# Reordering the opening and the hand-written slots of a sliding-window attention plus feed-forward kernel

## The chip, the cores and the metric

The kernel runs on one core of one Trainium2 chip. The metric is the device time of one execution in microseconds (us), shown as the median of several runs. One execution was also taken by the hardware profiler; all views below come from it. TensorE does the matmuls and weight loads, VectorE the masks, norms and statistics, ScalarE the exponentials, most casts and most of the ReLUs, GpSimd (POOL in the profile) and SyncE (SP) issue transfers.

## What is computed

```
q, k, v: [8, 8, 576, 64] fp32        # batch, heads, sequence, head size
rel    = pos[:, None] - pos[None, :]
scores = q @ k^T / sqrt(64) - slope[h] * |rel|, kept where 0 <= rel < 128
x      = softmax(scores) @ v, heads side by side -> [8, 576, 512]
xn     = (x - mean(x)) / sqrt(var(x) + 1e-6) * g_ln
out    = x + relu(xn @ w_ch1) @ w_ch2      # 512 -> 2048 -> 512, fp32 out
```

## The kernel before

The attention goes over 8 sequences ("b") of 4 head pairs ("hp") each, 32 pairs numbered n = 4b + hp. One pair needs its q, k and v in fp32 staging tiles (four deep, so pair n + 4 reuses the tile of pair n), a cast of each to fp16, and a transpose of q and k. For the pairs n below 10 (`PE_TURNS`) the transpose is a TensorE transpose (`turn_pe`) and a VectorE copy out of PSUM (`turn_out`); from pair 10 on it is a DMA transpose on the SP queue (`turn_dma`, L184). Then come two groups of score matmuls (`scores`, L249), an exponential for each group on ScalarE (`expo`), a multiplication with the decayed band mask on VectorE (`mask`), the product with v for each of the two heads (`pv`, L291) and the division by the row sum (`norm`). In the first sequence the second group's scores go to two single banks, and its exponential is two instructions.

After a sequence's fourth pair, five token blocks are normalised: `stats` (two VectorE instructions), `rstd` (two small ScalarE instructions), `scaled` (VectorE, L362, tile xs), and a transpose into the tile xt, on TensorE for sequences 0 and 1 (`xturn_pe`, copied out by ScalarE at L387) and by DMA on SP afterwards (`xturn_dma`, L374).

The feed-forward part goes over 9 chunks of 512 tokens. A chunk is 16 groups of four matmuls `m1` (L397, each followed by `relu`, every fourth one on VectorE) and 16 groups of four matmuls `m2` (L418, with `finish` adding x and storing). Chunk c needs xt of all its tokens: chunk 0 those of sequence 0, chunk 1 reaches into block 3 of sequence 1, chunks 2 and 3 reach into block 2 of sequences 2 and 3, chunks 4 and 5 into block 1 of sequences 4 and 5.

The order of the work is written by hand. Every operation is given a slot number through `at(t, fn, ...)`; one slot is about one group of four `m1` or `m2` matmuls. The list is sorted by slot and emitted inside `tc.manual_schedule()`, and each engine and queue executes its share in that order. `T0` is the slot of the first `m1`; `base(n)` is the slot at which pair n's scores start, and the other steps of the pair stand at fixed distances from it; `lead` is how many slots ahead of it the q and k casts stand. Slots set the order alone: an instruction starts when those ahead of it on its engine are done and its inputs are there.

The opening loads of the kernel before are outside that region, in the text ahead of it. There the order on a queue is chosen by the framework's scheduler: on the GpSimd queue the first quarter of W1 (`load_w1(0)`) and the tails of the second sequence's q and k came out ahead of the first sequence's v, and the rest of the second sequence's first pairs was mixed in between. The v loads carry an added dependency (`gated`) on the k load of their pair. Each load is two DMAs of 128 KB (tails one of 128 KB); each quarter of W1 and W2 is one of 512 KB in fp16. The GpSimd queue has eight completion semaphores, so that a DMA waits for the eighth before it to land.

`scale_w1` multiplies W1 by the gain g_ln in place, in 16 pieces.

Of the kernel before, what the change touches and what calls it, by code (L numbers as in the profile page):

```python
# [16 lines left out]
def kernel(  # L17
# [10 lines left out]
    nc = tc.nc  # L28
    B, H, S, D = q.shape
# [15 lines left out]
    inv_sqrt_d = float(1.0 / np.sqrt(D))  # L45
    eps = 1e-6
# [73 lines left out]
    def gated(d, gate):  # L120
        if gate is not None:
            tc.add_manual_dep(d.ins, gate.ins.name, SYNC, reason="load order")
        return d

    def load(n, b, hp, eng, gate=None):
        for g in range(2):
            d = eng.dma_start(  # L127
                out=stage[n][(b * HPAIRS + hp) % NSTG][:, :, g, :],
                in_=dram[n][b, 2 * hp + g, 0 : NFULL * P, :].rearrange("(sb p) d -> p sb d", p=P),
            )  # L130
            gated(d, gate)
        return d

    def load_tail(n, b, eng, gate=None):
        d = eng.dma_start(
            out=stage_t[n][b % 2][:, :, :],
            in_=dram[n][b, :, NFULL * P : S, :].rearrange("h p d -> p h d"),
        )
        return gated(d, gate)

    def load_w1(i):
        f0 = i * 512
        nc.gpsimd.dma_start(out=w1sb[:, :, f0 : f0 + 512], in_=w1r[:, :, f0 : f0 + 512])
# [297 lines left out]
    def at(t, fn, *args):  # L441
        todo.append((t, len(todo), fn, args))

    T0 = 29.5
    LAST = B * HPAIRS
    PE_TURNS = 2 * HPAIRS + 2

    def base(n):
        b, hp = divmod(n, HPAIRS)
        if b == 0:  # L450
            return 6.5 + 3.8 * hp
        if b == 1:
# [6 lines left out]
    nc.vector.memset(eps_t, eps)  # L459
    for i in range(2):  # L460
        nc.vector.memset(tail16["k"][i][TAIL:P, :, :], 0.0)
        nc.vector.memset(vext[i][:, :, :, D:VD], 1.0)
        nc.vector.memset(vext[i][TAIL:P, NSB - 1, :, :], 0.0)


    nc.scalar.dma_start(out=iden, in_=iden_dram.ap())
    kgate = {0: load("k", 0, 0, nc.scalar)}
    load_tail("k", 0, nc.scalar)
    nc.scalar.preload_act_table_set("natural_log_exp_and_others")
    load("q", 0, 0, nc.sync)  # L470
    load_tail("q", 0, nc.sync)
    for hp in range(HPAIRS):
        hs = slice(2 * hp, 2 * hp + 2)
        if hp > 0:
            load("q", 0, hp, nc.sync)
            kgate[hp] = load("k", 0, hp, nc.sync)
        nc.sync.dma_start(out=masks[:, hs, :], in_=m_dram.ap()[:, hs, :])
    nc.sync.dma_start(out=g_sb, in_=moe_g_ln.rearrange("(kb p) -> p kb", p=P))
    for hp in range(HPAIRS):
        load("v", 0, hp, nc.gpsimd, kgate[hp])  # L480
        if hp == 0:
            load_tail("v", 0, nc.gpsimd, kgate[hp])
    load_w1(0)

    def load_seq(b, hp):
        if hp == 0:
# [17 lines left out]
    for n in range(LAST):  # L504
        b, hp = divmod(n, HPAIRS)
        a = base(n)
        first = b == 0
        if hp == 0:
            at(a - 9.0, new_batch, b)
        if first:  # L510
            at(a - 2.2, cast, "q", b, hp, nc.scalar)
            at(a - 2.1, cast, "k", b, hp, nc.vector if hp == 0 else nc.scalar)
            ops = (-1.4, -1.0, -0.9, -0.5, -0.4)
            at(a + 1.95, cast_v, b, hp, nc.scalar)
            if hp == 0:
                at(a + 1.96, cast_v_tail, b, nc.scalar)
            e = (0.0, 0.3, 0.2, 1.0, 1.7, 2.7, 3.5, 3.7, 3.6, 3.9)
        else:
            lead = 3.6 if n < PE_TURNS else 8.0
            at(a - lead, cast, "q", b, hp, nc.scalar)  # L520
            at(a - lead + 0.05, cast, "k", b, hp, nc.vector)
            ops = (-2.4, -1.7, -3.5, -2.0, -1.3)
            at(a - 3.0, cast_v, b, hp, nc.scalar)
            if hp == 0:
                at(a - 2.95, cast_v_tail, b, nc.scalar)
            e = (0.0, 0.5, 2.6, 3.1, 2.0, 4.6, 6.3, 6.8, 7.2, 7.7)
        for x, m in ((0.0, "q"), (0.1, "k")):
            if n < PE_TURNS:
                at(a + ops[0] + x, turn_pe, m, b, hp)
                at(a + ops[1] + x, turn_out, m, b, hp)  # L530
            else:
                at(a - lead + 0.6 + x, turn_dma, m, b, hp)
            if hp == 0:
                teng = nc.scalar if m == "q" else nc.vector
                if n < PE_TURNS:
                    at(a + ops[2] + x, cast_tail, m, b, teng)
                    at(a + ops[3] + x, turn_tail_pe, m, b)
                    at(a + ops[4] + x, turn_tail_out, m, b)
                else:
                    at(a - lead + 0.1 + x, cast_tail, m, b, teng)  # L540
                    at(a - lead + 0.8 + x, turn_tail_dma, m, b)
        at(a + e[0], scores, b, hp, 0, False)
        at(a + e[1], expo, b, hp, 0, False)
        at(a + e[2], scores, b, hp, 1, first)
        at(a + e[3], expo, b, hp, 1, first)
        at(a + e[4], mask, b, hp, 0)
        at(a + e[5], mask, b, hp, 1)
        at(a + e[6], pv, b, hp, 0)
        at(a + e[7], norm, b, hp, 0)
        at(a + e[8], pv, b, hp, 1)  # L550
        at(a + e[9], norm, b, hp, 1)
        if hp == HPAIRS - 1:
            s = a + e[9] + 0.6
            if b % 2 == 1:
                at(s, move_half, b)
            u = 0.8 if first else 1.0
            for tb in range(NSB):
                at(s + u * tb, stats, b, tb)
                x = s + u * (2.9, 3.3, 4.9, 5.3, 6.0)[tb]
                at(x, scaled, b, tb)  # L560
                at(x + 0.3, xturn_pe if b <= 1 else xturn_dma, b, tb)
            at(s + u * 2.1, rstd, b, 0, 2)
            at(s + u * 4.1, rstd, b, 2, 4)
            at(s + u * 5.1, rstd, b, 4, 5)

    for c in range(NCHUNK):
        w = T0 + (NFB + 4 * CBLK) * c
        for fb in range(NFB):
            at(w + fb, m1, c, fb)
            at(w + fb + 0.95, relu, c, fb)  # L570
        for i in range(4 * CBLK):
            tb, f0 = divmod(i, 4)
            if c == 0:
                f0, tb = divmod(i, CBLK)
            at(w + NFB + i, m2, c, tb, 4 * f0)
            if f0 == 3:
                at(w + NFB + i + 0.95, finish, c, tb)
# [34 lines left out]
```

## Time and profile before

| | us |
|---|---|
| median of 13 runs | 377.44 |
| lowest and highest of them | 374.28, 380.69 |
| the profiled execution, its own time | 379.91 |
| span in its trace, first to last instruction | 378.1 |
| TensorE busy | 320.2 |
| VectorE busy | 202.9 |
| ScalarE busy | 190.6 |
| first `m1` matmul starts at | 48.6 |
| first `m1` of chunk 1, 2, 3, 4, 5 | 94.1, 138.1, 178.75, 215.3, 253.3 |

The profiled execution took 2.47 us more than the median of the runs. Of its own time 1.8 us lie outside the span. In the timeline a row is one instruction, or several alike that follow each other: start, duration, engine, line, operation, output and inputs, shapes, count, and in brackets the idle time of the engine before it with what ended it. The table by stretches gives, for each, its length and the busy time of each engine, then the mean clock granted to TensorE (1.00 is full speed), the mean busy share of the DMA engines and the rate that they moved.

### The profile page before, as it was taken

Reading aid. Unit: us, or ns where it says so; the run is one execution under the profiler, and the core shown is the slowest. Engines: PE = TensorE matmul, PEld = TensorE weight load, DVE = VectorE, ACT = ScalarE, POOL = GpSimd, SP = SyncE. Lnnn points to the kernel's source line nnn. Section 1 sums busy time; section 2 is a strip of 40 time slices with the busy share of each in tenths; the row PEclk is TensorE's granted clock in tenths of the full one; section 3 lists DMA queues with packets and bytes.
Section 4 is the critical chain, followed back from the end, with each engine's and each line's share of the span. In section 5 each row is a group of like instructions: output and inputs, shape, how many; then the busy total and the mean of one; then the engine's idle time right before and its main releaser. Section 6 shows DMA issues by size and latency. Waiting matters only on the chain.

```text
span 378.1 us, 6132 instructions
## 1 busy us (share of the span) xinstructions
PE 320.2 (85%) x2256; PEld 155.5 (41%) x2256; DVE 202.9 (54%) x460; ACT 190.6 (50%) x329; POOL 153.3 (41%) x210
## 2 busy tenths in 40 slices
PE   0354299986998949996999899969999999999995
PEld 0243144543444414442444344424444444444442
DVE  1456737667564935585366855855586557221221
ACT  2356769534785327741675477427745722511500
POOL 2739943795758334834366448344100000000000
PEclk9996579999899989997899999999999999999999
DMA  8997699669889993699469987997345106202002
GB/s 153 215 216 196 161 202 210 161 189 239 181 147 153 211 208 101 138 196 229 122 150 191 205 192 146 216 215 165 88 114 132 29 28 134 76 28 85 0 28 85
DMA packets 73309, 56.09 MB, mean 148 GB/s; under 512 B 57216, under 2 KB 61312, under 8 KB 73280
## 3 DMA queue, kind: packets, MB, share of 16 engines
q0 software_dynamic: 13728, 30.16, 38.9%
q1 hardware_dynamic: 57824, 25.12, 32.6%
q10 hardware_dynamic: 1728, 0.43, 0.7%
q8 instruction: 18, 0.29, 0.4%
q14 instruction: 11, 0.09, 0.1%
HBM read 37.78 MB, written 9.44 MB: 125 GB/s over the span
## 4 chain that ended last, share of the span: by engine, by line
PE 58%; DMA 18%; DVE 12%; POOL 3%; issue 3%; SPq 2%; ACT 2%; ACTq 0%; POOLq 0%
PE pm L397 31%; PE po L418 19%; DMA xt<-xs 6%; DMA kT<-k 5%; DVE st L333 4%; PE sc L249 3%; PE ppv L291 3%; DMA kt<-in_k_dram 3%; DMA w1sb<-in_moe_w_ch_dram 2%; DMA k<-in_k_dram 2%; DVE o L429 2%; DVE xs L362 2%; DVE pr L280 1%; SPq L127 1%; POOL v L127 1%
## 5 line engine op out<-in xcount | busy, mean ns | idle before, releaser
L397 PE MATMUL pm<-xt,w1sb 128*128 128x512 f16 x576 | 139.4, 390 | 8.7 <-DMA xt<-xs 8.7
L418 PE MATMUL po<-w2sb,ht 128*128 128x512 f16 x576 | 134.6, 382 | 0.0
L408 ACT ACTIVATE ht<-pm 128x512 f16<-128x512 f32 x108 | 64.4, 599 | 71.3 <-PE pm L397 71.2
L267 ACT ACTIVATE pr<-sc 128x1024 f16<-128x1024 f32 x60 | 61.4, 1023 | 47.1 <-PE sc L249 46.9
L397 PEld LDWEIGHTS <-w1sb 128*128 128x128 f16 x576 | 53.3, 99 | 73.2 <-issue 12.9
L418 PEld LDWEIGHTS <-ht 128*128 128x128 f16 x576 | 53.0, 98 | 60.7 <-issue 3.5
L127 POOL DMA_DIRECT2D v<-in_v_dram x64 | 47.7, 749 | 72.4 <-ACT vx L160 52.1
L280 DVE TENSOR_TENSOR pr<-pr,masks 128x1024 f16<-128x1024 f16 x64 | 43.8, 684 | 29.6 <-ACT pr L267 28.4
L127 POOL DMA_DIRECT2D k<-in_k_dram x56 | 41.8, 751 | 22.9 <-DVE k L162 16.8
L410 DVE TENSOR_SCALAR ht<-pm 128x512 f16<-128x512 f32 x36 | 24.9, 691 | 46.9 <-PE pm L397 46.7
L127 POOL DMA_DIRECT2D q<-in_q_dram x56 | 41.9, 753 | 16.0 <-ACT q L160 10.0
L429 DVE TENSOR_TENSOR o<-po,xp 128x512 f32<-128x512 f32 x36 | 24.6, 684 | 29.9 <-PE po L418 28.3
L291 PEld LDWEIGHTS <-pr 128*128 128x128 f16 x576 | 27.3, 101 | 20.7 <-DVE pr L280 4.2
L291 PE MATMUL ppv<-vx,pr 128*128 128x65 f16 x576 | 29.7, 198 | 6.5 <-ACT vx L160 4.3
L249 PE MATMUL sc<-qT,kT 64*128 64x256 f16 x240 | 23.4, 276 | 7.3 <-DMA kT<-k 7.1
L304 DVE RECIPROCAL rec<-ppv 128x5 f32<-128x5 f32 x64 | 12.2, 191 | 27.6 <-PE ppv L291 27.5
L339 ACT ACTIVATE rstd<-mv,eps_t 128x2 f32<-128x2 f32 (+1 forms) x24 | 7.0, 294 | 31.0 <-DVE mv L334 30.8
L249 PEld LDWEIGHTS <-kT 64*128 64x128 f16 x320 | 11.6, 100 | 25.1 <-issue 13.6
L160 ACT ACTIVATE q<-q 128x512 f16<-128x512 f32 x32 | 20.1, 627 | 2.6 <-DMA q<-in_q_dram 2.4
L160 ACT ACTIVATE vx<-v 128x512 f16<-128x512 f32 x32 | 20.0, 626 | 0.9 <-DMA v<-in_v_dram 0.9
L200 PE MATMUL ptr<-iden,q 128*128 128x128 f16 x40 | 4.8, 254 | 15.4 <-ACT q L160 15.4
L162 DVE CAST k<-k 128x512 f16<-128x512 f32 x29 | 12.5, 432 | 9.0 <-DMA k<-in_k_dram 9.0
(49 smaller groups left out, 198.8 us busy)
## 6 DMA issues: line engine op xcount, KB each, us to landing
out_dram<-o SPq DMA_DIRECT2D x36, 256.0 KB, 2.7
v<-in_v_dram POOLq DMA_DIRECT2D x64, 128.0 KB, 4.2
q<-in_q_dram POOLq DMA_DIRECT2D x56, 128.0 KB, 4.8
k<-in_k_dram POOLq DMA_DIRECT2D x56, 128.0 KB, 4.5
w1sb<-in_moe_w_ch_dram POOLq DMA_DIRECT2D x4, 512.0 KB, 8.3
w2sb<-in_moe_w_ch_dram POOLq DMA_DIRECT2D x4, 512.0 KB, 15.3
xp<-xo SPq DMA_DIRECT2D x4, 320.0 KB, 5.1
q<-in_q_dram SPq DMA_DIRECT2D x8, 128.0 KB, 7.8
```

The source lines that it names most:

```text
L127: d = eng.dma_start(out=stage[n][(b * HPAIRS + hp) % NSTG][:, :, g, :], in_=dram[n][b, 2 * hp + g, 0 : NFULL * P, :].rearrange("(sb p) d - ...
L160: nc.scalar.activation(out=out_, in_=in_, func=AF.Copy)
L249: nc.tensor.matmul(sc[g][:, OFF[j] + c0 : OFF[j] + c0 + n], kt[r, q0 : q0 + P] if j < NFULL else ktl[r, hp, :], src[r, col : col + n] if c ...
L267: nc.scalar.activation(out=pr[:, :, :], in_=c16_of.pop("sc")[:, :, :], func=AF.Exp, scale=inv_sqrt_d)
L280: nc.vector.tensor_tensor(out=view, in0=view, in1=m, op=ALU.mult)
L291: nc.tensor.matmul(ppv[:, qb, :], pr_of[b, hp, GRP[j]][:, g, off : off + P], vx[:, j, h, 0 : D + 1], start=(j == qb), stop=(j == max(qb - ...
L333: nc.vector.bn_stats(out=st[0:r, :], in_=xb_of[b][0:r, tb, :])
L397: nc.tensor.matmul(pm[:, :], w1sb[:, kb, fb * P : fb * P + P], xts[c][:, kb, :], start=(kb == 0), stop=(kb == NKB - 1),)
L408: nc.scalar.activation(out=hts[c][:, fb, :], in_=pm[:, :], func=AF.Relu)
L410: nc.vector.tensor_scalar(out=hts[c][:, fb, :], in0=pm[:, :], scalar1=0.0, scalar2=None, op0=ALU.max)
L418: nc.tensor.matmul(pms[c, "o", tb][:, :], hts[c][:, fb, tb * P : tb * P + P], w2sb[:, fb, :], start=(fb == 0), stop=(fb == NFB - 1),)
L429: nc.vector.tensor_tensor(out=o_tile[:, :], in0=pms.pop((c, "o", tb))[:, :], in1=xp_of[blk // PBLK][:, blk % PBLK, :], op=ALU.add,)
```

## The change

The opening loads and memsets become a function `opening()` at slot -100, so that they too are emitted in the written order. On the GpSimd queue this gives: v of all four pairs of the first sequence, each behind its k; all four quarters of W1; then the second sequence; then W2 as before. The q and k casts and the turns of the first sequence move up by 1.5 slots, which on ScalarE puts the casts of pair n + 1 ahead of the exponentials of pair n, and on TensorE its turns ahead of the `pv` of pair n. The v casts of pairs 1 and 3 of the first sequence go to VectorE; the second sequence's k casts go from VectorE to ScalarE. The first quarter of W1 is scaled on VectorE, behind the normalisation of the first sequence, instead of on ScalarE in the middle of it.

The second sequence's attention starts 5 slots later and is spaced 4.7 instead of 5.2 slots; the third's is spaced 5.5 instead of 6.5; from the fourth on the attention stands half a slot later. Every chunk from 1 on stands 2.5 slots later (`chunk_at`). `lead` for the pairs that are turned by DMA goes from 8 to 11 slots: the casts on ScalarE and VectorE and both DMA transposes on SP move up with it, ahead of the third and fourth xt transposes of the sequence that is being normalised. The normalisation of sequences 0 and 1 gets a denser order. The number and size of the instructions of each kind stay the same, apart from the casts and scalings that change their engine.

```diff
-    T0 = 29.5
+    T0 = 29.0
...
         if b == 0:
-            return 6.5 + 3.8 * hp
+            return 6.0 + 3.8 * hp
         if b == 1:
-            return T0 + 2.0 + 5.2 * hp
+            return T0 + 7.5 + 4.7 * hp
         if b == 2:
-            return T0 + 29.0 + 6.5 * hp
-        return T0 - 42.0 + 8.0 * n
+            return T0 + 30.5 + 5.5 * hp
+        return T0 - 41.0 + 8.0 * n
+
+    def chunk_at(c):
+        return T0 + (NFB + 4 * CBLK) * c + (3.0 if c else 0.0)
+
+    def opening():
...
+        for hp in range(HPAIRS):
+            load("v", 0, hp, nc.gpsimd, kgate[hp])
+            if hp == 0:
+                load_tail("v", 0, nc.gpsimd, kgate[hp])
+        for i in range(4):
+            load_w1(i)
+
+    at(-100.0, opening)
...
-    for i in range(1, 4):
-        at(base(HPAIRS - 1) + 2.1 + 0.01 * i, load_w1, i)
...
-            t = T0 - 5.0 if i == 0 else T0 - 1.2 + 3.45 * i
-            at(t + 0.1 * kb, scale_w1, i, kb, nc.scalar if i == 0 or kb % 2 else nc.vector)
+            t = T0 - 0.35 if i == 0 else T0 - 1.0 + 3.45 * i
+            at(t + 0.05 * kb, scale_w1, i, kb, nc.scalar if i and kb % 2 else nc.vector)
...
         if first:
-            at(a - 2.2, cast, "q", b, hp, nc.scalar)
-            at(a - 2.1, cast, "k", b, hp, nc.vector if hp == 0 else nc.scalar)
-            ops = (-1.4, -1.0, -0.9, -0.5, -0.4)
-            at(a + 1.95, cast_v, b, hp, nc.scalar)
+            at(a - 3.7, cast, "q", b, hp, nc.scalar)
+            at(a - 3.6, cast, "k", b, hp, nc.vector if hp == 0 else nc.scalar)
+            ops = (-2.9, -2.6, -2.4, -2.0, -1.9)
+            at(a + 1.3, cast_v, b, hp, nc.scalar if hp % 2 == 0 else nc.vector)
...
-            lead = 3.6 if n < PE_TURNS else 8.0
+            lead = 3.6 if n < PE_TURNS else 11.0
             at(a - lead, cast, "q", b, hp, nc.scalar)
-            at(a - lead + 0.05, cast, "k", b, hp, nc.vector)
+            at(a - lead + 0.05, cast, "k", b, hp, nc.scalar if b == 1 else nc.vector)
...
-            u = 0.8 if first else 1.0
+            if b <= 1:
+                st, sc, rs = (0.0, 0.8, 1.6, 2.5, 5.0), (2.0, 3.0, 3.3, 3.6, 6.0), (1.7, 2.95, 5.9)
+            else:
+                u = 1.0
+                st = [u * x for x in (0.0, 1.0, 2.0, 3.0, 4.0)]
+                sc = [u * x for x in (2.9, 3.3, 4.9, 5.3, 6.0)]
+                rs = [u * x for x in (2.1, 4.1, 5.1)]
...
-        w = T0 + (NFB + 4 * CBLK) * c
+        w = chunk_at(c)
```

More of the change, by code (lines that the diff above doesn't have):

```diff
@@ L450, in base @@
         if b == 0:
-            return 6.5 + 3.8 * hp
+            return 6.0 + 3.8 * hp
         if b == 1:
-            return T0 + 2.0 + 5.2 * hp
+            return T0 + 7.5 + 4.7 * hp
         if b == 2:
-            return T0 + 29.0 + 6.5 * hp
-        return T0 - 42.0 + 8.0 * n
[L459 to L463, printed above, removed]
@@ L466 @@
[L466 to L477, printed above, removed]
@@ L478 @@
[L478 to L483, printed above, removed]
+            return T0 + 30.5 + 5.5 * hp
[3 more added lines that the diff above has]
+    def opening():
+        nc.vector.memset(eps_t, eps)
+        for i in range(2):
+            nc.vector.memset(tail16["k"][i][TAIL:P, :, :], 0.0)
+            nc.vector.memset(vext[i][:, :, :, D:VD], 1.0)
+            nc.vector.memset(vext[i][TAIL:P, NSB - 1, :, :], 0.0)
+        nc.scalar.dma_start(out=iden, in_=iden_dram.ap())
+        kgate = {0: load("k", 0, 0, nc.scalar)}
+        load_tail("k", 0, nc.scalar)
+        nc.scalar.preload_act_table_set("natural_log_exp_and_others")
+        load("q", 0, 0, nc.sync)
+        load_tail("q", 0, nc.sync)
+        for hp in range(HPAIRS):
+            hs = slice(2 * hp, 2 * hp + 2)
+            if hp > 0:
+                load("q", 0, hp, nc.sync)
+                kgate[hp] = load("k", 0, hp, nc.sync)
+            nc.sync.dma_start(out=masks[:, hs, :], in_=m_dram.ap()[:, hs, :])
+        nc.sync.dma_start(out=g_sb, in_=moe_g_ln.rearrange("(kb p) -> p kb", p=P))
+        for hp in range(HPAIRS):
+            load("v", 0, hp, nc.gpsimd, kgate[hp])
[3 more added lines that the diff above has]
+            load_w1(i)
@@ L510 @@
         if first:
[L511 to L514 removed]
+            at(a - 3.7, cast, "q", b, hp, nc.scalar)
+            at(a - 3.6, cast, "k", b, hp, nc.vector if hp == 0 else nc.scalar)
+            ops = (-2.9, -2.6, -2.4, -2.0, -1.9)
+            at(a + 1.3, cast_v, b, hp, nc.scalar if hp % 2 == 0 else nc.vector)
             if hp == 0:
[L516 removed]
+                at(a + 1.35, cast_v_tail, b, nc.scalar)
             e = (0.0, 0.3, 0.2, 1.0, 1.7, 2.7, 3.5, 3.7, 3.6, 3.9)
         else:
[L519 removed]
+            lead = 3.6 if n < PE_TURNS else 11.0
             at(a - lead, cast, "q", b, hp, nc.scalar)
[L521 removed]
+            at(a - lead + 0.05, cast, "k", b, hp, nc.scalar if b == 1 else nc.vector)
             ops = (-2.4, -1.7, -3.5, -2.0, -1.3)
@@ L555 @@
                 at(s, move_half, b)
-            u = 0.8 if first else 1.0
-            for tb in range(NSB):
[L558 to L564, printed above, removed]
+            if b <= 1:
[5 more added lines that the diff above has]
+                rs = [u * x for x in (2.1, 4.1, 5.1)]
+            for tb in range(NSB):
+                at(s + st[tb], stats, b, tb)
+                at(s + sc[tb], scaled, b, tb)
+                at(s + sc[tb] + 0.3, xturn_pe if b <= 1 else xturn_dma, b, tb)
+            for x, c0, c1 in zip(rs, (0, 2, 4), (2, 4, 5)):
+                at(s + x, rstd, b, c0, c1)
     for c in range(NCHUNK):
-        w = T0 + (NFB + 4 * CBLK) * c
+        w = chunk_at(c)
         for fb in range(NFB):
```

## The prediction

> **What bounds the kernel now.** I read the page's slices first, then the chain of waits, then the table by stretches, then the timeline where a stretch is longer than its work.
>
> ```profile
> PE   0354299986998949996999899969999999999995
> PEclk9996579999899989997899999999999999999999
> L397 PE MATMUL pm<-xt,w1sb 128*128 128x512 f16 x576 | 139.4, 390 | 8.7 <-DMA xt<-xs 8.7
> ```
>
> TensorE is nearly full from slice 6 on, except for dips that come once per chunk, and several of these are followed by a dip of the clock. Ahead of slice 6 it is mostly idle. So there are two places to win: the 48.6 us ahead of the first `m1`, and the dips.
>
> ```profile
> 94.10:138.10 44.00, 36.60 (x287) 17.45 (x284) 27.46 (x62) 25.00 (x43) 27.35 (x37) 0.97 1.00 183
> 138.10:178.75 40.65, 36.12 (x249) 16.52 (x249) 22.58 (x51) 21.31 (x36) 18.77 (x26) 0.92 0.83 165
> 178.75:215.31 36.56, 35.14 (x249) 16.42 (x249) 22.15 (x51) 21.32 (x36) 19.84 (x27) 0.95 0.86 165
> 215.31:253.26 37.95, 33.81 (x249) 16.06 (x249) 23.75 (x55) 21.26 (x36) 20.08 (x27) 1.00 1.00 190
> 253.26:287.60 34.34, 33.74 (x250) 16.35 (x251) 22.74 (x53) 21.15 (x36) 7.43 (x10) 1.00 0.57 129
> ```
>
> Each row runs from one chunk's first `m1` to the next. The last four hold the same TensorE work, but take 40.65, 36.56, 37.95 and 34.34 us. The last, at full clock with 0.6 us idle, gives the clean length: 33.74. The first row has one `pv` pair, two turns and an xt turn more (0.54 + 0.46 + 0.23), so 35.0. The losses are 9.0, 6.9, 2.8, 4.2 and 0.6: **23.5 us**. From 287.6 to 318.9 TensorE is busy for 31.30 of 31.30 us, and behind that only matmuls run: nothing can be won there.
>
> ```profile
> 120.84 0.39 PE L249 MATMUL sc<-qT,kT 64*128 64x256 f16 x4 [1.13 <-DMA kT<-k]
> 138.08 1.86 PE L397 MATMUL pm<-xt,w1sb 128*128 128x512 f16 x4 [5.23 <-DMA xt<-xs]
> 174.21 0.39 PE L249 MATMUL sc<-qT,kT 64*128 64x256 f16 x4 [2.23 <-DMA kT<-k]
> 178.75 1.89 PE L397 MATMUL pm<-xt,w1sb 128*128 128x512 f16 x4 [1.31 <-DMA xt<-xs]
> 249.34 0.39 PE L249 MATMUL sc<-qT,kT 64*128 64x256 f16 x4 [1.78 <-DMA kT<-k]
> 253.26 1.04 PE L397 MATMUL pm<-xt,w1sb 128*128 128x512 f16 x4 [1.70 <-DMA xt<-xs]
> ```
>
> The losses are waits for DMA transposes of k and of xs (in all 7.1 and 8.7 us). The groups at 138.08 and 178.75 take 1.86 and 1.89 us where the one at 253.26 takes 1.04: there the clock is at half speed.
>
> **The change, part 1: the opening.** In the timeline of the first sequence, ScalarE and GpSimd show these rows:
>
> ```profile
> 28.06 1.02 ACT L267 ACTIVATE pr<-sc 128x1024 f16<-128x1024 f32 x1 [1.78 <-PE sc L249]
> 28.98 1.08 ACT L263 ACTIVATE pr<-sch 128x512 f16<-128x512 f32 x2
> 29.20 1.49 POOL L127 DMA_DIRECT2D v<-in_v_dram  x2 [2.40 <-DMA k<-in_k_dram]
> 29.94 0.64 ACT L160 ACTIVATE q<-q 128x512 f16<-128x512 f32 x1
> 40.12 2.54 ACT L152 ACTIVATE w1sb<-w1sb,g_sb 128x512 f16<-128x512 f16 x4
> ```
>
> Pair 3's casts stand behind pair 2's exponentials, its turns behind its casts, and pair 2's `pv` behind those turns. Scores start at 14.4, 22.1, 27.4 and 32.6. With casts and turns ahead, a pair costs 0.65 (scores) + 2.1 (exponentials) + 0.7 (mask) + 0.9 (rest of `pv`), 4.3 us, instead of 5.2, if its loads are there. They set the pace: each exponential now also waits for the next pair's k. GpSimd's waits show k of pairs 1, 2, 3 landing at 15.2, 23.1 and 29.2. By then W1's first quarter (0.52 MB) and tails of sequence 2 (0.26 MB) had passed, and for the last two also its third tail and parts of its first pair (0.52 MB more). The stretches show 203 to 230 GB/s; at 217 these 0.78 and 1.30 MB are 3.6 and 6.0 us. So k lands at 11.6, 17.1 and 23.2 at the latest; the last by bytes at 22.7, which I take. Then: two casts, 1.2 us (23.9); pair 2's exponentials (26.0); mask (26.7); `pv`; pair 3's scores at 27.6. From scores to `stats` was 32.6 to 37.95, 5.35 us, less 0.15 with the v cast on VectorE: 32.8.
>
> From `stats` to the first `m1` was 10.7 us, with the 2.54 us of W1 scaling shown above in the middle of it on ScalarE, and casts and turns of sequence 2 at its end. Now: three `stats` (0.82 each), `rstd` (0.5), two `scaled` (0.42), wait for the second `rstd`, two `scaled`, about 5.5 us; transposes, copies and the last small block, to 8.0; the first W1 piece, 0.35. First `m1` at 32.8 + 8.4 = 41.2: **7.4 us gained**. W1 is issued behind v of pair 3, from about 24.5, with 2.1 MB landing by some 36; not late.
>
> Sequence 2's loads now wait behind W1 on GpSimd's queue and semaphores, from about 36.5, at 0.75 us per DMA. Its first q and k land near 40; their casts stand behind three `m1` groups, at 45. W2 is issued near 50 (46.6 before); its first quarter is wanted after sixteen groups, above 60. Both cost nothing; if this cover failed, the delay would be theirs in full, 2 to 5 us.
>
> A rule speaks against moving casts and scalings to VectorE. W1's four issues took 0.75 to 1.06 us each on GpSimd (median 0.84), partly beside VectorE's casts, W2's four 0.76 to 0.79. The Trainium skill ("SBUF — State Buffer", "Who interferes with whom") says that a VectorE copy or scaling in a two-port mode shuts GpSimd out for the whole instruction. By the rule the two v casts (0.43 each) and four scalings (0.35) add up to 2.3 us to the queue; by the rows, at most 0.3 for each, 1.8. Either is inside the slack of the paragraph above: I add nothing, with 2.3 kept for the range.
>
> **Part 2: chunk 0.** The stretch from first `m1` to chunk 1's took 45.5 us. It takes over the turns of sequence 2's first pair with its tails (0.9) and those of the third sequence's second pair (0.5). ScalarE takes four k casts more (0.64 each) beside 12 ReLUs; it was 94% busy from 60 to 70 us, so I add 1.3, between 0 and 2.6. At the end, the last `pv` used to be followed by 8.7 us of TensorE work in 13.7 us; now by three `m2` groups, scores, turns and xt turns, 4.6, while VectorE has 8.4 us of norm, four `stats`, four `scaled`, three `finish` and a mask, then about 2 us for the last turn and copy: idle 5.8 instead of 5.0, so 0.8. Sum **3.5 us lost**.
>
> **Part 3: chunks 1 to 5.** The chunks move 2.5 slots back, the attention half a slot: two slots more between xs and its chunk, and 4.5 for chunk 2. A slot is 0.86 us, with the attention between about 1.05. The chain from the last `pv` of a sequence to xt's landing is about 14 us; TensorE now has 13 us of work for it, against 8 at chunk 2 and 11 at chunk 3. Remainders: 1.4 at chunks 2 and 3, 0.7 at chunk 5. The DMA transposes of q and k stand 3 slots earlier; the waits for them were 0.8 to 2.2 us, so they go. They are moved past the third or fourth xt transpose on SP (1.2 us to issue each), which no chunk is waiting for next. Casts standing earlier on ScalarE must find their loads there: the load of a pair waits for a cast some 30 slots ahead of it and takes 4.8 us to land, so they do. Waits for masks stay, 2.0.
>
> Half clock is the last term. By the stretch of 178 to 182 us the granted clock was 0.50, and it had fallen in 174 to 178 (0.66) behind an idle of only 2.23. The skill ("TensorE: Matmul & The Clock Gate", "What's actually happening") has the gate fall to half after an idle window of about 3.4 us. By the rule remainders of 1.4 us never cost clock; by the rows they may. I take one such stretch, 1.3 us (1.86 for 1.04, and the next group's part); the rule would make it 0.
>
> What is left is 1.4 + 1.4 + 0.7 + 2.0 + 1.3 = 6.8 of 23.5; with the 0.5 of turns that moved ahead, **17.2 us gained**.
>
> **Sum**: -7.4 + 3.5 - 17.2 = -21.1 us. The profiled execution's 379.9 becomes 358.8; it stood 2.5 above the median of the runs, so against 377.4 the kernel takes **356 us**.
>
> **The rivals.**
> *The opening stays bound by issue, not bytes.* SP's own issues wait for space (2.0 to 4.05 us for some masks and loads), so k of pair 3 could land at 27 in spite of fewer bytes. Then `m1` starts near 46 and 2.5 of the 7.4 us are left: 361. For it: SP's long issues[...].
> *The stalls come back at the chunks.* With k's waits gone TensorE arrives earlier and waits for xt instead; VectorE is busy for 12.2 of 20 us there, in one piece. If half of the 23.5 remain, 5 us more than I leave: 361 to 366.
> *Slower: ScalarE blocked by early casts.* 22 pairs' q casts stand three slots earlier, ahead of ReLUs and exponentials. If a load is not there, ScalarE stops, PSUM fills and TensorE with it, up to three slots (2.6 us) per pair, 57 us: 413. It decides from 1 us per pair on, 21 us, which eats the gain. Against it: the trace shows only 2.4 us of q casts waiting for loads, all at the first pair.
>
> **How the numbers follow.** My forecast 0.70 (348 to 362 alone), the opening's rival 0.12, the stalls' 0.12, the slower one 0.05; 0.01 that gains and losses cancel. The range 346 to 367 takes in the first three with the 2.3, 2.6 and 5 us of the unknown costs; outside it lie the slower case and the rest of the tails. About 0.3% is what a measurement of this kernel can tell from no change. Faster 0.93, same 0.01, slower 0.06.
>
> **What would show it.** Right: first `m1` near 41, no wait for kT above 0.5 us, waits for xt at chunks 2 and 3 under 2 us, stretches between chunks of 34 to 36 us. Wrong: a first `m1` behind 46, q casts that wait for loads on ScalarE, stretches that stay at 38 or more, or W2's first quarter holding the first `m2`.

## The result, and the profile after

The changed kernel takes 365.7 us (median of 11 runs, 362.3 to 373.6) against 377.4 us for the kernel before in the same comparison: a ratio of 0.968 [0.965, 0.971], 11.7 us less. Ratios here leave out executions over 1.5% above the fastest of their kernel. The forecast was 356 us, 21.4 less, so little more than half of the forecast gain came. The range up to 367 held the time with 1.3 us to spare; it lies outside the 348 to 362 that the prediction gave to its own account alone.

The profiled pair shows more. The changed kernel's profiled execution took 362.81 us, 2.9 below its median; that of before took 379.91, 2.5 above. So the two traces lie 17.1 us apart (spans 378.1 and 361.0), the medians 11.7. Both differences need an explanation, and they have different ones.

The slices and the costliest group on the changed kernel's page:

```profile
PE   1662789995999998998999999989999999999995
PEclk9999999996799999999999999999999999999999
L397 PE MATMUL pm<-xt,w1sb 128*128 128x512 f16 x576 | 137.0, 386 | 2.1 <-DMA xt<-xs 1.5
```

TensorE is at work from slice 5 on instead of slice 6. The one deep dip left is slice 10, the end of chunk 0, and there and in slice 11 the clock still falls (0.6 and 0.7). The waits for xt shrank from 8.7 to 1.5 us.

The changed kernel's table by stretches (length, busy time of PE, PEld, DVE, ACT and POOL, granted clock, DMA share, GB/s), from one chunk's first `m1` to the next, chunks 0 to 5. The DMA share adds up the times of all packets; they overlap, so it can pass 1.00.

```profile
39.75:91.00 51.25, 43.96 (x340) 22.55 (x341) 32.69 (x76) 33.84 (x59) 41.39 (x56) 0.93 0.92 200
91.00:128.48 37.48, 36.67 (x282) 16.98 (x282) 25.11 (x59) 23.50 (x42) 28.30 (x38) 0.96 1.17 210
128.48:165.69 37.21, 33.67 (x249) 16.16 (x248) 24.06 (x55) 21.41 (x37) 20.07 (x27) 1.00 1.13 192
165.69:199.96 34.27, 33.43 (x248) 16.14 (x248) 21.11 (x50) 20.84 (x36) 20.17 (x27) 1.00 1.05 184
199.96:234.56 34.60, 33.51 (x249) 16.18 (x248) 22.43 (x52) 21.13 (x37) 20.04 (x27) 1.00 1.12 198
234.56:270.64 36.08, 33.58 (x249) 16.16 (x248) 22.82 (x53) 21.16 (x37) 5.93 (x8) 1.00 0.72 128
```

First `m1` came 8.9 us earlier (39.75 for 48.6), chunk 0 got 5.8 longer (51.25 for 45.5), and the five stretches from chunk 1 on 13.6 shorter (179.6 for 193.2). The prediction's last row ends at 287.60, but chunk 6's first `m1` stood at 287.31 in the kernel before; hence 193.2. Those three terms make 16.7 of the 17.1, and 0.4 came behind them. Note the DMA column: in four of the five stretches from chunk 1 on it is now above 1.0, with the traffic of before squeezed into less time.

What TensorE waited for, changed kernel (us in total, times, longest):

```profile
PE ppv L291 <- DVE pr L280: 8.1, 10, 1.5
...
PE sc L249 <- DMA kT<-k: 3.1, 4, 1.2
PE pm L397 <- DMA xt<-xs: 1.5, 1, 1.5
```

### The profile page after: what moved, and what is told of

It is laid out like the page before. It is cut to its first block, busy times and chain, and to the rows that moved or that the text cites. A ratio compares the mean times of both kernels' runs of the same rounds, so it can differ in the third digit from the quotient of the medians.

```text
span 361.0 us, 6117 instructions
## 1 busy us (share of the span) xinstructions
PE 318.4 (88%) x2256; PEld 156.2 (43%) x2256; DVE 201.9 (56%) x462; ACT 189.5 (52%) x327; POOL 153.4 (42%) x210
## 3 DMA queue, kind: packets, MB, share of 16 engines
HBM read 37.78 MB, written 9.44 MB: 131 GB/s over the span
## 4 chain that ended last, share of the span: by engine, by line
PE 58%; DMA 22%; DVE 9%; ACT 5%; SPq 2%; issue 2%; POOL 1%; ACTq 0%
PE pm L397 27%; PE po L418 24%; DMA kT<-k 12%; PE ppv L291 3%; PE sc L249 3%; DVE st L333 3%; DMA q<-in_q_dram 3%; DMA xt<-xs 2%; DMA kt<-in_k_dram 2%; DMA w1sb<-in_moe_w_ch_dram 2%; DMA k<-in_k_dram 2%; DVE pr L280 1%; DVE o L429 1%; ACT ht L408 1%; ACT vx L160 1%
## 5 line engine op out<-in xcount | busy, mean ns | idle before, releaser
L397 PE MATMUL pm<-xt,w1sb 128*128 128x512 f16 x576 | 137.0, 386 | 2.1 <-DMA xt<-xs 1.5
L418 PE MATMUL po<-w2sb,ht 128*128 128x512 f16 x576 | 132.7, 379 | 0.0
L408 ACT ACTIVATE ht<-pm 128x512 f16<-128x512 f32 x108 | 62.9, 595 | 50.5 <-PE pm L397 50.4
L127 POOL DMA_DIRECT2D v<-in_v_dram x64 | 48.5, 761 | 81.5 <-ACT vx L160 58.4
L280 DVE TENSOR_TENSOR pr<-pr,masks 128x1024 f16<-128x1024 f16 x64 | 43.4, 680 | 10.5 <-ACT pr L267 9.5
L291 PE MATMUL ppv<-vx,pr 128*128 128x65 f16 x576 | 30.6, 199 | 13.4 <-DVE pr L280 8.1
L249 PEld LDWEIGHTS <-kT 64*128 64x128 f16 x320 | 11.6, 99 | 20.5 <-issue 12.9
L160 ACT ACTIVATE vx<-v 128x512 f16<-128x512 f32 x30 | 18.7, 625 | 0.0
L305 DVE TENSOR_TENSOR xo<-ppv,rec 128x320 f16<-128x320 f32 x32 | 15.7, 492 | 1.1
L305 DVE TENSOR_TENSOR xp<-ppv,rec 128x320 f16<-128x320 f32 x32 | 15.7, 491 | 1.1
```

The costliest lines, as they stand in the source:

```text
L127: d = eng.dma_start(out=stage[n][(b * HPAIRS + hp) % NSTG][:, :, g, :], in_=dram[n][b, 2 * hp + g, 0 : NFULL * P, :].rearrange("(sb p) d - ...
L160: nc.scalar.activation(out=out_, in_=in_, func=AF.Copy)
L249: nc.tensor.matmul(sc[g][:, OFF[j] + c0 : OFF[j] + c0 + n], kt[r, q0 : q0 + P] if j < NFULL else ktl[r, hp, :], src[r, col : col + n] if c ...
L280: nc.vector.tensor_tensor(out=view, in0=view, in1=m, op=ALU.mult)
L291: nc.tensor.matmul(ppv[:, qb, :], pr_of[b, hp, GRP[j]][:, g, off : off + P], vx[:, j, h, 0 : D + 1], start=(j == qb), stop=(j == max(qb - ...
L305: nc.vector.tensor_tensor(out=xb_of[b][:, 0:NSB, D * h : D * h + D], in0=ppv[:, :, 0:D], in1=rec[:, :].unsqueeze(2).broadcast_to([P, NSB, D]),
```

## The experiments

All were run in five rounds, in three groups of four, each beside the kernel before. "Changed kernel's" numbers are those above unless the repeat is named. Under "sum" stands the total of the five stretches from chunk 1's first `m1` to chunk 6's.

**Only the order of the loads.** The kernel before with the opening loads in the written order, all of W1 among them; no other slot moved.

```diff
+    def opening():
...
+        for i in range(4):
+            load_w1(i)
+    at(-100.0, opening)
...
-    for i in range(1, 4):
-        at(base(HPAIRS - 1) + 2.1 + 0.01 * i, load_w1, i)
```

> The kernel before with one part alone: the opening loads written out in the slot order (v of the first sequence behind its k, then all of W1, then the second sequence); casts, turns and all slots as before. Mine: k of pairs 1, 2, 3 lands some 4 to 7 us earlier, but the casts still stand behind the exponentials (5.2 us per pair), and the second sequence's turns, which stand ahead of the first m1, now wait for loads behind W1. First m1 near 44 to 46, total 2 to 4 us below before (ratio 0.990 to 0.995). Rival 1, the order is the whole gain of the opening: first m1 near 40, ratio 0.98. Rival 2, the second sequence's late loads take it all back: first m1 at 48 or later, ratio 1.00 or above.

371.9 us, 6.95 less than before, ratio 0.983 [0.978, 0.988]; more than expected. First `m1` at 43.4. So the order of the loads alone is 5.2 of the 8.9 us of the opening. Chunk 0 took 45.1 and the sum is 193.8, both within 0.6 us of before.

**The whole opening, without the slots.** To that are added the earlier casts and turns of the first sequence, its v casts and W1's first scaling on VectorE. Slots of all later work as before.

```diff
-            at(a - 2.2, cast, "q", b, hp, nc.scalar)
+            at(a - 3.7, cast, "q", b, hp, nc.scalar)
...
-            ops = (-1.4, -1.0, -0.9, -0.5, -0.4)
+            ops = (-2.9, -2.6, -2.4, -2.0, -1.9)
```

> The kernel before with the whole of the opening's part: load order, casts and turns of the first sequence 1.5 slots earlier, v casts of pairs 1 and 3 and the scaling of W1's first quarter on VectorE; everything from the second sequence on in its old slots. Mine: first m1 near 41 (39.75 after the full change, 48.6 before), the stretches between chunks stay as before (44, 40.7, 36.6, 38.0), so about 7 us are gained, ratio 0.982. Rival, the gain is given back in chunk 0 because the second sequence's loads and W2 now come later: chunk 1 starts no earlier than 92, ratio 0.995 to 1.0.

374.4 us, 4.5 less than before, ratio 0.988 [0.983, 0.993], and first `m1` at 44.2 instead of 41: a miss. VectorE's and TensorE's timelines in this run, just ahead of the first `m1`:

```profile
41.12 0.62 DVE L162 CAST k<-k 128x512 f16<-128x512 f32 x1 [2.16 <-DMA k<-in_k_dram]
41.99 1.49 DVE L154 TENSOR_SCALAR w1sb<-w1sb,g_sb 128x512 f16<-128x512 f16 x4
41.80 0.61 PE L200 MATMUL ptr<-iden,k 128*128 128x128 f16 x4 [0.40 <-DVE k L162]
43.87 0.37 PE L217 MATMUL ptrt<-iden,qt 64*128 64x64 f16 x4 [1.46 <-DVE qT L207]
```

These are the turns of the *second* sequence's first pair. In the old slots they stand ahead of the first `m1` on TensorE; their loads now come behind all of W1, and the copy of the first turn stands behind W1's scaling on VectorE. The change moves that sequence five slots back, and only with that move do the earlier casts pay.

**Only the slots.** The opening of before, with all later slots, `lead` and the normalisation order as changed.

```diff
-            return T0 + 2.0 + 5.2 * hp
+            return T0 + 7.5 + 4.7 * hp
...
+        return T0 + (NFB + 4 * CBLK) * c + (3.0 if c else 0.0)
...
-            lead = 3.6 if n < PE_TURNS else 8.0
+            lead = 3.6 if n < PE_TURNS else 11.0
```

> The other part alone: the new slots of sequences 2 and on, of the chunks, the lead of 11 and the denser normalisation; the opening (loads, casts, turns, scaling of W1's first quarter) as before. Mine: the stretches between chunks 1 to 6 are those after the full change (37.5, 37.2, 34.3, 34.6, 36.1), 14 us shorter than before, while chunk 0 takes about 4 us more: ratio 0.974 to 0.978. Rival, the chunks only looked long because TensorE ran at half clock there, and the opening is what counts: ratio 0.99 or above.

373.0 us, 5.9 less, ratio 0.984 [0.979, 0.989], less than expected. First `m1` at 47.6, chunk 0 took 50.8, sum 180.4. Chunk 0's loss (5.3) and the later gain (12.8) both come from the slots; they are there without the opening. The two halves of the change don't add up at the first `m1`: alone they bring it 4.4 and 1.0 us forward, together 8.9.

**Lead 8 in the changed kernel.** Casts and DMA transposes of q and k three slots later again.

```diff
-            lead = 3.6 if n < PE_TURNS else 11.0
+            lead = 3.6 if n < PE_TURNS else 8.0
```

> The changed kernel with the lead of the casts and DMA transposes back at 8 slots. Mine: the waits for kT, 3.1 us in the changed kernel, go back to some 6 to 7 us, and the time to 3 or 4 us above the changed kernel (ratio to before 0.977). Rival, the transposes are late because the DMA engines are full (they land 6 to 10 us after issue there), and the waits seen are made by that and by VectorE's late k casts: three slots decide little, within 1 us of the changed kernel (ratio 0.967 to 0.971).

372.6 us, only 6.3 less than before, ratio 0.979 [0.973, 0.985]. In its trace the waits for kT were 4.6 us (3.1 in the changed kernel), those for masks 9.7 (8.1), and one of 1.25 for a cast of q's tail was new: with the 0.5 less at xt 3.9 of the 5.2 us between the two spans. All six executions (368.0 to 376.1) are longer than 12 of the 17 of the changed kernel and its repeat. The lead is worth 4 us by the ratios and 5.4 by the medians, and less of it than expected shows as waits for kT.

**Chunks from 2 on two slots earlier in the changed kernel.**

```diff
-        return T0 + (NFB + 4 * CBLK) * c + (3.0 if c else 0.0)
+        return T0 + (NFB + 4 * CBLK) * c + ((1.0 if c > 1 else 3.0) if c else 0.0)
```

> The changed kernel with chunks 2 to 8 two slots earlier, so that attention and chunks stand to each other as in the kernel before from the fourth sequence on; chunk 1 keeps its 3 slots. Mine: the xt waits come back, some 1.5 to 2 us at each of chunks 2, 3 and 5, with half clock behind some of them: stretches 1 to 3 and 5 longer by 1 to 2 us each, 4 to 6 us in all, ratio to before 0.979 to 0.984. Rival, the lead and the spacing of sequences 2 and 3 do the work and the shift of the chunks is slack: within 1.5 us of the changed kernel (0.967 to 0.972).

370.1 us, 7.9 less than before, ratio 0.974 [0.968, 0.980]: 3.8 us of the gain gone by the medians, 2.3 by the ratios, whose intervals overlap. Its trace is its slowest execution (374.6 us); sum 189.7. TensorE's timeline in it, at the first `m1` of chunks 2, 3 and 5:

```profile
133.21 1.87 PE L397 MATMUL pm<-xt,w1sb 128*128 128x512 f16 x4 [3.84 <-DMA xt<-xs]
174.29 1.89 PE L397 MATMUL pm<-xt,w1sb 128*128 128x512 f16 x4 [3.83 <-DMA xt<-xs]
246.47 1.04 PE L397 MATMUL pm<-xt,w1sb 128*128 128x512 f16 x4 [2.02 <-DMA xt<-xs]
```

The wait for xt is back at all three, and the groups behind the first two run at half speed (1.87 and 1.89 us; a group at full clock takes 1.0). For chunks 2 and 5 the two slots are what shortened or removed it: the ten traces with the distance of the change wait at most 2.8 us at chunk 2 and never at chunk 5. For chunk 3 this run shows nothing: five of those ten wait there for 3.5 to 5.3 us.

**Second sequence back to its old slots in the changed kernel.**

```diff
-            return T0 + 7.5 + 4.7 * hp
+            return T0 + 2.0 + 5.2 * hp
```

> The changed kernel with the second sequence's pairs back at T0 + 2.0 + 5.2 hp, 5.5 slots earlier for the first pair and 4 for the last. Mine: chunk 0, 51.25 us after the change against 45.5 before, gets its 4 to 5 us back at its end, where the last pv had too little TensorE work behind it; but the turns of the second sequence stand ahead of the first m1 again and wait for loads behind W1, so the first m1 starts at 43 to 45 instead of 39.75: in all within 1.5 us of the changed kernel. Rival 1, only the end of chunk 0 counts: ratio to before 0.955 to 0.960. Rival 2, only the first m1 counts: 0.978 to 0.982.

367.3 us, ratio 0.966 [0.958, 0.972]. First `m1` went to 44.5, chunk 0 fell to 47.7; chunk 1 started at 92.2, against 91.0. What the first `m1` lost, chunk 0 won.

**W1's first scaling and all v casts of the first sequence back on ScalarE, in the changed kernel.**

```diff
-            at(t + 0.05 * kb, scale_w1, i, kb, nc.scalar if i and kb % 2 else nc.vector)
+            at(t + 0.05 * kb, scale_w1, i, kb, nc.scalar if i == 0 or kb % 2 else nc.vector)
...
-            at(a + 1.3, cast_v, b, hp, nc.scalar if hp % 2 == 0 else nc.vector)
+            at(a + 1.3, cast_v, b, hp, nc.scalar)
```

> The changed kernel with the first sequence's v casts and the scaling of W1's first quarter on ScalarE, in the same slots, instead of VectorE. It tests the rule that VectorE's copies hold up the GpSimd queue. Mine: GpSimd's issues stay at 0.75 us each and the queue is no earlier; the first m1 is 1 to 2 us later because four scalings of 0.7 us take the place of four of 0.35 and ScalarE's copies of xt stand ahead of them; ratio 0.970 to 0.974. Rival (the rule): GpSimd issues W1 and the second sequence up to 2.3 us earlier, and chunk 0 is shorter by about as much: 0.962 to 0.966.

368.6 us, ratio 0.976 [0.970, 0.981]. First `m1` came at 39.9 and chunk 0 took 51.7, so the place named for a loss isn't one. The sum is 183.8 against 179.6, and these 4 us stand at chunk 3's first `m1`:

```profile
167.69 2.29 PE L397 MATMUL pm<-xt,w1sb 128*128 128x512 f16 x5 [3.50 <-DMA xt<-xs]
```

The changed kernel waits for 1.52 us there, and without the half clock that follows here for 6.8 us. The edit touches nothing near chunk 3, the same wait comes in other variants (below), and the executions (365.0 to 369.8) lie among those of the changed kernel: a loss by the edit is not shown. W1's four issues on GpSimd took 0.77 to 0.80 us in both kernels, but in neither did a cast or scaling on VectorE run beside them, so they say nothing on the rule.

**The first pair's second mask moved ahead in the slots**, from the third sequence on, before steps of the previous sequence's normalisation on VectorE.

```diff
-        at(a + e[5], mask, b, hp, 1)
+        at(a + (3.8 if b > 1 and hp == 0 else e[5]), mask, b, hp, 1)
```

> The changed kernel with one thing more: for the first pair of every sequence from the third on, the second group's mask stands 0.8 slots earlier on VectorE, ahead of the last stats and a finish. In the changed kernel TensorE waits 0.80 to 0.85 us once per chunk at this pair's pv for that mask. Mine: these five waits go, 3 to 4 us, ratio to before 0.958 to 0.961. Rival, xs and xt come later by as much and TensorE waits there, or arrives earlier at the same transposes of k: within 1 us of the changed kernel.

368.4 us (360.0 to 371.9), 9.6 less than before; the ratio, 0.957 [0.950, 0.965], rests on its few lowest executions. Waits for masks fell from 8.1 to 3.9 us, but waits for xt rose from 1.5 to 7.3 in the trace. That the mask now delays the normalisation was not tested, and similar waits for xt come without this edit. Inconclusive as a gain.

**The changed kernel once more**, in the third group.

> The changed kernel itself once more, so that the kernels of this group and of the two before can be set against it on one chip. Mine: ratio to before 0.965 to 0.972, and stretches within 1.5 us of those of its first profile (51.3, 37.5, 37.2, 34.3, 34.6, 36.1), first m1 at 39.7. Rival, the executions of this kernel spread by several us because waits for DMA transposes come and go: the first m1 and chunk 0 stay, but single stretches between chunks move by 2 us or more.

366.0 us, 12.8 less than before in that group, ratio 0.958 [0.953, 0.964]; single executions from 361.8 to 371.8. Its trace, a span of 360.0 us, agrees: first `m1` at 38.8, chunk 0 51.8, sum 179.1. The same pair of kernels gave 0.968 in the first comparison, outside this interval, while the medians, 365.7 and 366.0, agree: a difference of 1% between ratios of different groups shows nothing by itself.

**The changed kernel without the v loads of the last five sequences**, 5.24 MB of 37.78 read from memory. Their `pv` works on what the buffers hold. All casts, matmuls and stores stay.

```diff
-        for n in "qkv":
+        for n in ("qkv" if b < 3 else "qk"):
```

> The changed kernel without the v loads of the fourth to eighth sequence (their pairs compute with the v already in the staging tiles), some 5 MB less for the DMA engines; all instructions of the compute engines and all transposes stay. Mine: the DMA engines, over 100% busy in these stretches, make the transposes of k and xs land late; with a third of the loads gone kT lands in 4 to 5 us (median 5.9 in the changed kernel), and stretches 2 to 5 come to 34.0 to 34.5 us, 2 to 4 us less in all: ratio to before 0.957 to 0.962. Rival, what is left is VectorE's order alone: stretches as in the changed kernel, ratio within 0.004 of it.

359.6 us, 19.2 less than before and 6.4 less than the repeat beside it, ratio 0.949 [0.945, 0.953]; by the ratios it is 3.6 us ahead of the repeat. All six executions (358.1 to 361.3) are shorter than all 17 of the changed kernel and its repeat (361.8 to 373.6). The stretch of chunk 2, first of the repeat and then of this run:

```profile
130.00:166.30 36.30, 33.59 (x248) 16.14 (x249) 22.38 (x53) 21.13 (x36) 20.05 (x27) 1.00 1.08 192
128.40:162.70 34.30, 33.47 (x249) 16.20 (x250) 22.24 (x52) 20.87 (x36) 14.19 (x19) 1.00 0.83 174
```

Two waits for xt, 3.1 us in the repeat, are gone but for 0.4, and one for kT of 2.40 us came, so the sums, 179.1 and 178.0, are close in these two quick executions. The xt transposes' time from issue to landing, this run:

```profile
DMA to landing us min/median/max: 2.3/2.5/5.7
```

In the repeat the same answer is 2.3, 4.0 and 7.0. The transposes of q and k gained less: a median of 4.6 us for 5.6, and their longest still took 12.8.

**Second sequence half way back, two of the third's k casts on ScalarE.**

```diff
-            return T0 + 7.5 + 4.7 * hp
+            return T0 + 5.0 + 4.7 * hp
...
-            at(a - lead + 0.05, cast, "k", b, hp, nc.scalar if b == 1 else nc.vector)
+            at(a - lead + 0.05, cast, "k", b, hp, nc.scalar if b == 1 or n in (9, 10) else nc.vector)
```

> The changed kernel with the second sequence 2.5 slots earlier (T0 + 5.0 + 4.7 hp), so that its first turns still stand behind the first m1 groups, and with the k casts of the third sequence's second and third pair on ScalarE, out of VectorE's chain from the last pv to chunk 1. Mine: the first m1 stays at 39.7 to 40.5, and chunk 0 takes 47.5 to 49 us instead of 51.3: ratio to before 0.959 to 0.963. Rival, ScalarE becomes the bound of chunk 0 (59 instructions, 33.8 of 51 us): no gain, within 0.003 of the changed kernel.

367.0 us, ratio 0.969 [0.965, 0.974]; chunk 0 took 53.4 instead of getting shorter. TensorE's waits for q casts rose from 5.1 to 8.2 us. No gain.

**Both that and the earlier mask.**

> The two amendments together on the changed kernel: the second sequence 2.5 slots earlier with two k casts on ScalarE, and the mask of each first pair ahead of the last stats and a finish. Mine: chunk 0 at 47.5 to 49 us, the pv waits for masks below 5 us in all, ratio to before 0.952 to 0.958, median near 361. Rival, TensorE arrives earlier at the same transposes and waits there for what it saved: as seq2_mid or the changed kernel, 0.961 or above.

365.1 us (363.1 to 367.2), ratio 0.964 [0.959, 0.968], beside 366.0 for the repeat: not to be told from the changed kernel. No version that clearly beats it came out of these runs.

## Why the prediction was right, and where its steps were off

**The opening: right, 8.9 us for 7.4.** Loads pace it, as the byte count had it. GpSimd's, VectorE's and TensorE's rows in the changed kernel's timeline:

```profile
10.84 1.50 POOL L127 DMA_DIRECT2D v<-in_v_dram  x2 [2.18 <-DMA k<-in_k_dram]
16.94 1.48 POOL L127 DMA_DIRECT2D v<-in_v_dram  x2 [4.60 <-DMA k<-in_k_dram]
21.01 1.49 POOL L127 DMA_DIRECT2D v<-in_v_dram  x2 [2.58 <-DMA k<-in_k_dram]
31.55 0.69 DVE L333 BATCH_NORM_STATS2 st<-xp 128x6 f32<-128x512 f16 x1
39.75 6.99 PE L397 MATMUL pm<-xt,w1sb 128*128 128x512 f16 x24
```

The v issues start where k has landed: 10.8, 16.9 and 21.0 for the 11.6, 17.1 and 22.7 predicted. The last landing was 1.7 us better, and from there the steps hold: `stats` at 31.55 (32.8 predicted), 8.2 us on to `m1` (8.4 predicted). The load order alone gives 5.2 us of this; the rest needs casts, turns and the second sequence's move together. The rival with the opening bound by issue, `m1` near 46, is out.

**Chunk 0: the term that was mis-sized, 5.8 us lost for 3.5.** Chunk 0 in two parts, its `m1` groups and what follows up to chunk 1's first `m1`, in the kernel before and in the changed kernel:

```profile
48.62:70.50 21.88, 21.33 (x167) 10.32 (x166) 12.76 (x33) 17.99 (x31) 8.10 (x12) 0.91 1.16 200
70.50:94.10 23.60, 19.36 (x159) 9.69 (x157) 16.29 (x40) 9.05 (x19) 19.45 (x27) 0.98 0.78 196
```
```profile
39.75:61.56 21.81, 20.48 (x138) 9.63 (x139) 11.97 (x28) 19.11 (x34) 19.11 (x26) 1.00 0.85 180
61.56:91.00 29.44, 23.48 (x203) 12.91 (x202) 20.72 (x48) 14.73 (x26) 22.27 (x30) 0.88 0.98 215
```

(The clock record of the changed kernel starts at 43.1; ahead of it the `m1` matmuls are as slow as in the first 3.8 us of before.) The `m1` part holds 29 matmul records fewer and yet is as long. But they were small: TensorE's work there fell by 0.85 us only, and its idle time rose by 0.8, for the most part two waits of 0.29 and 0.60 us for VectorE's copies of the second sequence's turns, now among the `m1` groups. ScalarE was busy for 19.1 of the 21.8 us, but TensorE's one wait of over 0.15 us for it took 0.20. The work that was moved lengthens the second part.

Over the whole chunk TensorE's work grew by 3.3 us, where 1.4 had been put for the turns, and its idle time by 2.5, where 2.1 had been put (1.3 for ScalarE and 0.8 at the end). So the excess is in the work, and the clock explains most of it. The changed kernel at chunk 0's end and in chunk 1's first 3.3 us:

```profile
80.64:84.05 3.41, 1.61 (x10) 0.42 (x8) 3.34 (x8) 1.53 (x3) 3.41 (x6) 1.00 0.91 213
84.05:87.46 3.41, 1.15 (x12) 0.73 (x12) 3.34 (x10) 1.90 (x5) 2.17 (x3) 0.50 1.02 251
87.46:90.88 3.42, 2.69 (x20) 2.15 (x21) 2.03 (x6) 2.44 (x6) 2.26 (x3) 0.50 1.22 235
90.88:94.29 3.41, 3.29 (x11) 0.94 (x11) 1.58 (x5) 1.95 (x6) 2.45 (x3) 0.50 1.08 147
```

For 10.2 us the clock was at half; before it was so for 3.4 us there, from 93.4 on. TensorE worked for 3.8 of these us in chunk 0, an estimated 1.9 us longer than at full clock (0.4 before), and for 3.3 in chunk 1, 1.6 longer. The prediction had put its half clock behind a wait for xt and nothing here. What idles TensorE there is VectorE, with waits of 2.63 and 1.52 us for xs; it was busy for 6.7 of the 6.8 us from 80.64 on: two k casts at 81.63 and 86.16 (0.55 and 0.42 us) stand among `stats` and `scaled` and were left out of the 8.4 us. Moving the second sequence back doesn't help: chunk 1 started between 90.0 and 93.1 us in every variant of the changed kernel.

**Chunks 1 to 5: right in mechanism, 13.6 us for 17.2.** The waits for xt shrank, and those at chunks 2 and 5 come back when the distance is taken away. Of the prediction's clean length (169.5 in all) 10.1 us are still lost in the changed kernel's trace, where 6.8 was predicted: about 4.1 for masks, 3.1 for kT, 1.5 for xt and 1.6 for the half clock that chunk 1 inherits. TensorE's rows with idle time, three of them:

```profile
122.83 0.36 PE L291 MATMUL ppv<-vx,pr 128*128 128x65 f16 x6 [0.80 <-DVE pr L280]
142.15 0.39 PE L249 MATMUL sc<-qT,kT 64*128 64x256 f16 x4 [1.19 <-DMA kT<-k]
239.77 0.39 PE L249 MATMUL sc<-qT,kT 64*128 64x256 f16 x4 [1.05 <-DMA kT<-k]
```

A mask wait of 0.8 to 0.85 us stands once in each of the five stretches, 4.1 us where 2.0 had been put. And kT waits of 3.1 us where none had been: "so they go" was wrong. They became shorter, not absent, because the transposes now land later. All DMA transposes of q and k in the changed kernel, from issue to landing:

```profile
DMA to landing us min/median/max: 2.3/5.9/10.5
```

Before, the median was 4.8. The one behind the wait at 142.15 was issued at 132.66 and took 9.44 us. The three slots bought some 2.6 us (an estimate, at the 0.86 us of a slot), and the later landing took part of that back.

**What the sum left out: the other 5 to 6 us, between the traces' 17.1 and the medians' 11.7.** The steps together made 17.1 us in the traces for 21.1: 1.5 more at the opening hide part of the 2.3 and 3.6 that were missing behind it. The rest is that the prediction took its difference from one execution and set it on a median. It allowed for the 2.5 us by which that execution stood above the median of before; the changed kernel's profiled execution lies 2.9 below its own. No long execution of the changed kernel was profiled, so what grows in it wasn't seen. The other traces show a likely place: the wait at chunk 3's first `m1`, which was put at 1.4 us. It ends with one DMA transpose, the first into chunk 3 from the third block of sequence 3. In kernels with the distance of the change and a lead of 11, opening and all:

| trace | its own time, us | issue to landing, us | wait at chunk 3, us |
|---|---|---|---|
| without v loads | 360.2 | 3.2 | none |
| changed kernel | 362.8 | 6.2 | 1.5 |
| its repeat | 361.8 | 7.0 | 1.9 |
| both amendments | 364.3 | 7.8 | 3.8 |
| casts back on ScalarE | 367.6 | 8.2 | 3.5 |
| second sequence early | 370.4 | 8.8 | 3.7 |
| mask moved ahead | 368.4 | 9.0 | 5.3 |
| second sequence half way | 369.8 | 9.3 | 4.5 |

Behind the waits of 3.5 us and more the clock was at half for 3.4 or 6.8 us, and behind the shorter ones it was not; a longer wait and its half clock make 4 us in the casts' run. So the remainder for xt, 1.5 for 3.5 in the changed kernel's trace, was small because that execution was a good one, and that is luck. Without 5.24 MB of v loads the landing takes 3.2 us, the wait is gone and the median falls by 6.4. That run also takes those DMAs' issues off GpSimd (14 us busy per stretch for 20), so bytes and issues aren't told apart; and why the landing differs from one execution to the next at the same bytes stays open.

**The rivals.** The time lies in the range of the second, stalls coming back at the chunks (361 to 366). Waits for xt of 3.5 to 5.3 us, as five variants have them, are what it names; that they stand behind the changed kernel's median is likely and not shown. The reason that it gave, VectorE's busy stretch, wasn't tested by itself. The slower rival didn't come: q casts on ScalarE waited 4.6 us for loads in the whole span, 1.64 at most behind the opening, where it would have taken 21.

**VectorE beside GpSimd.** The prediction charged nothing for VectorE's casts and scalings beside GpSimd's issues. The time shows no cost, but the two do hold each other up. Two like casts in the changed kernel, the second beside GpSimd's issues:

```profile
18.92 0.42 DVE L162 CAST vx<-v 128x512 f16<-128x512 f32 x1
27.07 0.75 DVE L162 CAST vx<-v 128x512 f16<-128x512 f32 x1
27.48 0.84 POOL L127 DMA_DIRECT2D q<-in_q_dram  x1
```

In the 14 traces, 558 casts and scalings on VectorE within SBUF, the on-chip memory, and without an issue beside them took 0.43 us at most; of 616 with one, 205 took more than 0.45, up to 0.75. VectorE's copies of turns out of PSUM, TensorE's output memory, took 0.43 at most in both cases. Issues lengthen less: in the changed kernel 13 of the 47 beside such an instruction took more than 0.79 us, up to 0.96, and 1 of the other 159. So the traces agree with "SBUF — State Buffer", "Who interferes with whom", of the Trainium skill, where whichever of the two comes first blocks the other; the added 0.33 us is less than a whole issue. The prediction had looked at one direction only, and the dearer one here is VectorE's.

**The clock.** In all 14 traces the granted clock changes on a grid of 3.41 us steps. It fell 30 times, each time behind a step in which TensorE was busy for 47% or less; of 1222 full-clock steps that kept it, three lay at 41 to 47% and all others above. It came back behind steps of 89% and more. Steps of the kernel before, with 1.18 and 1.64 us busy, in the first and the last row; the clock fell behind the first (middle row) and not behind the last:

```profile
171.86:175.27 3.41, 1.18 (x12) 0.50 (x9) 0.02 (x1) 0.63 (x1) 1.23 (x2) 1.00 1.34 258
175.27:182.10 6.83, 5.52 (x21) 1.72 (x20) 3.12 (x8) 1.82 (x3) 1.48 (x2) 0.50 1.01 215
246.94:250.36 3.42, 1.64 (x19) 0.84 (x18) 0.53 (x1) 0.59 (x1) 1.74 (x3) 1.00 0.87 218
```

The first holds the wait of 2.23 us, the last that of 1.78. "TensorE: Matmul & The Clock Gate", "What's actually happening", of the Trainium skill has the fall behind an idle window of about 3.4 us; here a window that is less than half busy was enough, and the measurement decides. So a wait of 2 us costs clock or not by where it falls on the grid and what else is idle in its step.

## What to carry to other kernels

When work is moved out of a stretch, ask how much of the bounding engine's time it holds: 29 small matmuls were 0.85 us, as much idle time came in their place, and the part that received them grew by 5.8. Look at the end of that part too, where a step less than half busy costs the clock of the next ones. Two edits that meet in one engine's queue can't be costed apart; ask what stands ahead of the instruction that is to start earlier. And when stalls are removed the same bytes go through in less time: look at the DMA share of the stretches, take landing times from a loaded queue, and profile more than one execution before a trace's gain is set on a median.

## What was not expected of the hardware

With the DMA share of the stretches from 1.1 down to 0.8, the median landing of xt's transposes fell from 4.0 to 2.5 us, and every execution became shorter than every one with the full loads. At the same bytes the landing of one transpose differed from 6.2 to 9.3 us between traces, and the wait behind it from 1.5 to 5.3. Nor had it been expected that the clock falls behind 3.41 us of which TensorE works for up to 47%.
